# Fused cosformer attention and squared-ReLU MLP: one planner orders all engines, seven block products in the first matmul too

## The chip, the cores and the metric

The kernel runs on one NeuronCore of a Trainium2 chip. Five engines work in parallel, each through its own queue in order: TensorE (PE, matmuls, with its weight loads shown as PEld), VectorE (DVE), ScalarE (ACT), GpSimd (POOL) and SyncE (SP). In this kernel POOL and SP issue the DMA transfers, POOL on the software queue and SP on the hardware queue. Engines wait for one another on semaphores. The metric is the device time of one execution in microseconds (us).

## The reference, cut to what matters

There are 8 batches of 8 heads, 576 positions and 64 features per head. Attention is linear: both q and k go through a ReLU and are then multiplied by a cosine and by a sine of the position, which gives 128 features.

```
r = np.maximum(x, 0.0)
phi(x) = np.concatenate([r * c, r * s], axis=-1)
kv  = einsum('bhsf,bhsd->bhfd', phi(k), v);  z = sum(phi(k), axis=2)
num = einsum('bhsf,bhfd->bhsd', phi(q), kv); den = einsum('bhsf,bhf->bhs', phi(q), z) + 1e-06
x   = (num / den) as [8*576, 512]
out = (relu(x @ w_in) ** 2) @ w_out          # w_in [512, 2048], w_out [2048, 512]
```

Inputs and output are float32. The two large matmuls have 4608 x 512 x 2048 multiplications each and take nearly all of the time.

## The kernel before, in words

A batch of 576 positions is cut into four tiles of 128 (positions 4p + j, so that a partition reads whole rows) and one tail of 64. Weights are cast to bf16 by their load on the POOL queue. q, k and v come as float32, with two buffers each (`inp`, `bufs=2`), and v is cast by ACT or DVE into `vext` (`att_v`, L203 and L205), whose 65th column is 1 and so also gives z.

Per batch: features of k and q (`feat_cos` on DVE L176, `feat_sin` on ACT L186), the sums `kz` over positions (`att_kv`, L246), the copy to `kvz` (L257), the transpose of q (on PE for batches 0 and 1, by DMA from SP otherwise, L275), the numerators `num` (L318), the division on DVE (L328 to L332) and the transpose of x (PE L359 or DMA L350).

The first matmul (`gemm1`, L391) is done plainly, 16 matmuls of 256 columns into one PSUM tile `hps` (two banks, two such tiles). ACT writes relu to `rt` (L399), DVE squares into `gT` (L406). The tails of two batches are done together, 128 columns at a time.

The second matmul is plain for batch 0 (L440) and for half of batch 1 (L464). Otherwise a pair of 128-position tiles is done as a 2 x 2 block product with seven products instead of eight (`pair_mm`, L533): sums of g blocks on DVE (`g_sum`, L529), sums of w_out blocks once (`w2_sum`, L514), and the results are put together by ACT copies (L569, L584) and DVE adds (L545). A pair has four PSUM tiles `ya`, `yc`, `yv`, `yu`, one for each open sum. Tails go the same way, four batches at a time.

The order is written by hand: a list of slots (`gemm1` and `gemm2` pieces of one batch after the other), and tables (`plan`, `at`) that say behind which slot each attention piece is issued. Every engine then executes its own instructions in that order. Output goes from the POOL queue, 512 KB at a time (L418, tails L427), in the last batch from SP and ACT.

Of the kernel before, what the change touches and what calls it, by code (L numbers as in the profile page):

```python
# [14 lines left out]
EPS = 1e-06  # L15
FP = 512


@with_exitstack
def kernel(  # L20
# [15 lines left out]
    T = B * S  # L36
# [6 lines left out]
    assert P == 128 and H * D == 512 and D == 64 and TAIL == 64  # L43
    NS = J + 1

    const = ctx.enter_context(tc.tile_pool(name="const", bufs=1))
    wpool = ctx.enter_context(tc.tile_pool(name="wts", bufs=1))
    inp = ctx.enter_context(tc.tile_pool(name="inp", bufs=2))
    att = ctx.enter_context(tc.tile_pool(name="att", bufs=1))
    mlp = ctx.enter_context(tc.tile_pool(name="mlp", bufs=2))  # L50
    ps_h = ctx.enter_context(tc.tile_pool(name="ps_h", bufs=2, space=bass.MemoryType.PSUM))
    ps_y = ctx.enter_context(tc.tile_pool(name="ps_y", bufs=2, space=bass.MemoryType.PSUM))
    ps_a = ctx.enter_context(tc.tile_pool(name="ps_a", bufs=1, space=bass.MemoryType.PSUM))
# [3 lines left out]


    kqv = {}

    def load_main(src, nm, b, eng, parts=1):
        main = inp.tile([P, H, J, D], F32, name=nm, tag=nm, bufs=2)
        for i in range(parts):
            js = slice(i * J // parts, (i + 1) * J // parts)
            eng.dma_start(
                out=main[:, :, js, :],
                in_=src[b, :, 0:MAIN, :].rearrange("h (p j) d -> p h j d", j=J)[:, :, js, :],
            )
        kqv[nm, b] = main

    def load_tail(src, nm, b, eng):
        tail = inp.tile([P, HH, D], F32, name=nm + "t", tag=nm + "t", bufs=2)
        for g in range(2):
            eng.dma_start(
                out=tail[g * TAIL : (g + 1) * TAIL, :, :],
                in_=src[b, g * HH : (g + 1) * HH, MAIN:S, :].rearrange("h p d -> p h d"),
            )
        kqv[nm + "t", b] = tail

    def load_batch(b, eng, order):  # L80
        for nm in order:
            for part in (load_main, load_tail):
                part({"k": k, "v": v, "q": q}[nm], nm, b, eng)

    def piece(nm, b, j):
        return kqv[nm, b][:, :, j, :] if j < J else kqv[nm + "t", b][:, :, :]


    ident = const.tile([P, P], BF16, name="ident")
    zeros = const.tile([P, FP], BF16, name="zeros")  # L90
# [24 lines left out]


    w1sb = wpool.tile([P, KB, DFF], BF16, name="w1sb")
    w2sb = wpool.tile([P, HB, DM], BF16, name="w2sb")
# [16 lines left out]
    vexts = []  # L135
    for i in range(2):
        vx = att.tile([P, J, H, E1], BF16, name=f"vext{i}")
        vxt = att.tile([P, HH, E1], BF16, name=f"vextt{i}")
        for t in (vx, vxt):
            ones = t[:, :, :, D:E1] if t is vx else t[:, :, D:E1]  # L140
            nc.vector.memset(ones, 1.0)
        vexts.append((vx, vxt))
    kps, kvzs, kzs, qps, tqs, qpTs, xs = {}, {}, {}, {}, {}, {}, {}
    nums, xts, xtails = {}, {}, {}

    def cached(tiles, key, shape, tag, bufs):
        if key not in tiles:
            tiles[key] = att.tile(shape, BF16, name=tag, tag=tag, bufs=bufs)
        return tiles[key]


    def kp_of(b, j):
        if j == J:
            return cached(kps, (b, 1), [P, HH, F], "kpt", 1)
        return cached(kps, (b, 0), [P, J, H, F], "kp", 1)[:, j]

    def qp_of(b, j):
        if j == J:
            return cached(qps, (b, 2), [P, HH, F], "qpt", 2)
        return cached(qps, (b, j // 2), [P, 2, H, F], "qp", 2)[:, j % 2]  # L160

    def x_of(b, j):

        if j == J:
            return cached(xs, (b, 2), [P, 2, P], "xt", 2)
        return cached(xs, (b, j // 2), [P, KB, 2, P], "x", 2)[:, :, j % 2, :]

    def xT_of(b, i):
        return cached(xts, (b, i), [P, KB, 2 * P], "xT", 3)

    def xT_tails(m):

        return cached(xtails, m, [P, 2, 2, 2, TAIL], "xTt", 2)

    def feat_cos(dst, src, j):
        nc.vector.tensor_scalar(  # L176
            out=dst[:, :, 0:D],
            in0=src,
            scalar1=0.0,
            scalar2=cos_col[:, j : j + 1],  # L180
            op0=ALU.max,
            op1=ALU.mult,
        )

    def feat_sin(dst, src, j):
        nc.scalar.activation(  # L186
            out=dst[:, :, D:F], in_=src, func=ACTF.Relu, scale=sin_col[:, j : j + 1]
        )

    def feat_cos_act(dst, src, j):  # L190
        nc.scalar.activation(
            out=dst[:, :, 0:D], in_=src, func=ACTF.Relu, scale=cos_col[:, j : j + 1]
        )

    def att_k(b, j, cos=feat_cos):
        for f in (cos, feat_sin):
            f(kp_of(b, j), piece("k", b, j), j)

    def att_v(b, j, eng, h0=0, h1=H):
        copy = eng.copy if eng is nc.scalar else eng.tensor_copy  # L200
        vx, vxt = vexts[b % 2]
        if j == J:
            copy(out=vxt[:, :, 0:D], in_=piece("v", b, j))  # L203
        else:
            copy(out=vx[:, j, h0:h1, 0:D], in_=piece("v", b, j)[:, h0:h1, :])  # L205

    def warm(n):

        wm = ps_h.tile([P, 2, FP], F32, name="wm", tag="hps", bufs=2)
        for i in range(n):  # L210
            nc.tensor.matmul(
                out=wm[:, i % 2, :], lhsT=zeros[:, 0:P], rhs=zeros[:, :], start=True, stop=True
            )

    def fill(n):

        wm = ps_a.tile([P, 2, FP], F32, name="wm", tag="pa", bufs=1)
        for i in range(n):
            nc.tensor.matmul(
                out=wm[:, i % 2, :],  # L220
                lhsT=ident[:, :],
                rhs=zeros[:, :],
                start=True,
                stop=True,
            )

    def att_kv(b, part):
        vx, vxt = vexts[b % 2]
        if part == 0:
            kvzs[b] = att.tile([P, H, E1], BF16, name="kvz", tag="kvz", bufs=2)  # L230
            kzs[b] = ps_a.tile([P, 2, FP], F32, name="kz", tag="pa", bufs=1)
        kz = kzs[b]

        for j in (0, 1) if part == 0 else range(2, NS):
            for hh in range(HH):
                for half in range(2):
                    h = half * HH + hh  # L240
                    if j < J:
                        lhsT, rhs = kp_of(b, j)[:, h, :], vx[:, j, h, :]
                    else:
                        p0, p1 = half * TAIL, (half + 1) * TAIL
                        lhsT, rhs = kp_of(b, j)[p0:p1, hh, :], vxt[p0:p1, hh, :]
# [7 lines left out]
        if part == 1 and b:  # L253
            att_kvz(b, nc.scalar.copy)
# [223 lines left out]

# [337 lines left out]
```

## Time and profile before

| what | value |
|---|---|
| time, three executions | 288.13 us median (287.29 to 288.22) |
| profiled execution: first to last instruction | 286.5 us |
| median less that span (start and end of the execution) | 1.6 us |
| PE, PEld busy | 279.0, 235.6 us |
| DVE, ACT, POOL busy | 204.2, 161.8, 45.7 us |
| PE instructions | 3067 |
| data moved by DMA | 53.04 MB |

The profiled execution's own time is not given beside its span; the 1.6 us is the median's distance from the span. "Busy" is the time in which an engine had an instruction of its own under way. A matmul row's duration of 0.273 us includes its way through the array; two that follow each other start 0.109 us apart, so work on PE is counted by starts or by the chain of waits, not by durations. In the view in order of time, a bracket shows how long the engine was idle before a row and what ended that.

### The profile page before, as it was taken

What the parts mean: (1) busy time and instruction counts of PE and PEld (TensorE: products, weight loads), DVE (VectorE), ACT (ScalarE), POOL (GpSimd) and SP (SyncE); (2) the same over time, 40 slices, a digit from 0 to 9 for tenths busy, and PEclk for the clock granted to TensorE, in tenths of its full rate; (3) what the DMA queues carried; (4) which work ended last, traced back from release to release, by engine and by line L of the source; (5) the groups of instructions that cost most, each with busy time, mean ns of one, the idle gap of its engine ahead of it and who ended that gap; (6) DMA issues with size and microseconds to landing.
All of it is one profiled execution on the core that took longest, in us unless ns stands there. A gap on an engine that the chain in (4) does not pass through costs nothing.

```text
span 286.5 us, 7327 instructions
## 1 busy us (share of the span) xinstructions
PE 279.0 (97%) x3067; PEld 235.6 (82%) x3067; DVE 204.2 (71%) x457; ACT 161.8 (56%) x245; POOL 45.7 (16%) x75
## 2 busy tenths in 40 slices
PE   8899999999999999999999999999999999999995
PEld 3578855888678888889988988888988888889884
DVE  1857664688697599787598776977677877547585
ACT  3764833679669669445881458844695461155210
POOL 8925507640000000000002000000000000000002
PEclk9999999999999999999999999999999999999999
DMA  7999996999457898999439975499809620300015
GB/s 236 298 206 302 329 263 197 362 364 277 57 119 187 212 275 195 237 301 212 136 106 192 348 160 165 107 267 287 227 9 237 114 46 3 140 9 2 0 76 146
DMA packets 73825, 53.04 MB, mean 185 GB/s; under 512 B 50496, under 2 KB 68416, under 8 KB 73792
## 3 DMA queue, kind: packets, MB, share of 16 engines
q1 hardware_dynamic: 63248, 26.75, 40.4%
q0 software_dynamic: 10400, 25.69, 29.8%
q8 instruction: 24, 0.39, 0.6%
q10 hardware_dynamic: 144, 0.13, 0.1%
q14 instruction: 9, 0.07, 0.1%
HBM read 36.70 MB, written 9.44 MB: 161 GB/s over the span
## 4 chain that ended last, share of the span: by engine, by line
PE 86%; DMA 5%; POOL 3%; DVE 2%; ACT 2%; issue 1%; POOLq 0%; ACTq 0%
PE hps L391 40%; PE ya L533 9%; PE yc L533 9%; PE yu L533 7%; DMA w1sb<-in_moe_w_in_dram 5%; PE yv L533 5%; PE num L318 3%; PE kz L246 3%; PE yps L464 2%; PE yps L440 2%; PE yh L440 2%; DVE ysb L545 1%; PE tq L292 1%; POOL w1sb L122 1%; DVE u L545 1%
## 5 line engine op out<-in xcount | busy, mean ns | idle before, releaser
L391 PEld LDWEIGHTS <-w1sb 128*128 128x128 bf16 x1344 | 113.4, 98 | 13.3 <-issue 2.0
L391 PE MATMUL hps<-xT,w1sb 128*128 128x256 bf16 (+1 forms) x1088 | 119.3, 266 | 1.2 <-DMA w1sb<-in_moe_w_in_dram 0.4
L399 ACT ACTIVATE rt<-hps 128x1024 bf16<-128x1024 f32 x72 | 73.7, 1023 | 68.1 <-PE hps L391 46.7
L406 DVE TENSOR_TENSOR gT<-rt 128x1024 bf16<-128x1024 bf16 x64 | 44.0, 687 | 20.1 <-ACT rt L399 20.1
L533 PEld LDWEIGHTS <-gs 128*128 128x128 bf16 x480 | 46.9, 98 | 5.4
L418 POOL DMA_DIRECT2D out_dram<-ysb x14 | 7.6, 541 | 171.6 <-DVE ysb L545 144.9
L533 PEld LDWEIGHTS <-gT 128*128 128x128 bf16 x312 | 29.8, 98 | 3.4
L332 DVE TENSOR_TENSOR x<-num,rden 128x512 bf16<-128x512 f32 x32 | 22.1, 692 | 1.1
L186 ACT ACTIVATE kp<-k,sin_col 128x512 bf16<-128x512 f32 x32 | 22.4, 717 | 0.6 <-DMA k<-in_k_dram 0.6
L186 ACT ACTIVATE qp<-q,sin_col 128x512 bf16<-128x512 f32 x32 | 22.0, 719 | 1.1 <-DMA q<-in_q_dram 1.1
L328 DVE TENSOR_SCALAR den<-num 128x8 f32<-128x8 f32 (+1 forms) x40 | 6.6, 164 | 20.6 <-PE num L318 20.4
L529 DVE TENSOR_TENSOR gs<-gT 128x1024 bf16<-128x1024 bf16 x26 | 17.8, 684 | 0.0
L533 PE MATMUL ya<-w2t,gs 128*128 128x256 bf16 x120 | 15.6, 273 | 0.0
L533 PE MATMUL yc<-w2sb,gs 128*128 128x256 bf16 x120 | 15.6, 273 | 0.0
L533 PE MATMUL yu<-w2t,gs 128*128 128x256 bf16 x120 | 15.6, 272 | 0.0
L391 PE MATMUL hps<-xTt,w1sb 128*128 128x128 bf16 x256 | 15.1, 219 | 0.2 <-ACT rt L399 0.2
L176 DVE TENSOR_SCALAR qp<-q,cos_col 128x512 bf16<-128x512 f32 x32 | 14.7, 487 | 0.0
L533 PE MATMUL yu<-w2sb,gs 128*128 128x256 bf16 x112 | 14.5, 273 | 0.0
L205 ACT CAST vext<-v 128x512 bf16<-128x512 f32 x23 | 14.1, 614 | 0.6 <-DMA v<-in_v_dram 0.6
L584 ACT COPY s<-yu 128x256 f32<-128x256 f32 x14 | 5.2, 372 | 15.6 <-PE yu L533 15.6
L176 DVE TENSOR_SCALAR kp<-k,cos_col 128x512 bf16<-128x512 f32 x21 | 10.1, 504 | 5.0 <-DMA k<-in_k_dram 5.0
L533 PE MATMUL yc<-w2sb,gT 128*128 128x256 bf16 x104 | 13.5, 273 | 0.0
(98 smaller groups left out, 340.8 us busy)
## 6 DMA issues: line engine op xcount, KB each, us to landing
out_dram<-ysb POOLq DMA_DIRECT2D x14, 512.0 KB, 4.1
k<-in_k_dram SPq DMA_DIRECT2D x5, 1024.0 KB, 7.9
v<-in_v_dram POOLq DMA_DIRECT2D x4, 1024.0 KB, 8.6
v<-in_v_dram SPq DMA_DIRECT2D x4, 1024.0 KB, 8.7
q<-in_q_dram SPq DMA_DIRECT2D x4, 1024.0 KB, 6.7
q<-in_q_dram POOLq DMA_DIRECT2D x3, 1024.0 KB, 12.7
k<-in_k_dram POOLq DMA_DIRECT2D x3, 1024.0 KB, 10.0
w1sb<-in_moe_w_in_dram POOLq DMA_DIRECT2D x4, 512.0 KB, 11.2
```

The costliest lines, as they stand in the source:

```text
L176: nc.vector.tensor_scalar(out=dst[:, :, 0:D], in0=src, scalar1=0.0, scalar2=cos_col[:, j : j + 1], op0=ALU.max, op1=ALU.mult,)
L186: nc.scalar.activation(out=dst[:, :, D:F], in_=src, func=ACTF.Relu, scale=sin_col[:, j : j + 1])
L205: copy(out=vx[:, j, h0:h1, 0:D], in_=piece("v", b, j)[:, h0:h1, :])
L246: nc.tensor.matmul(out=kz[:, half, hh * E1 : (hh + 1) * E1], lhsT=lhsT, rhs=rhs, start=(j == 0 and hh == 0), stop=(j == J and hh == HH - 1),)
L318: nc.tensor.matmul(out=out, lhsT=lhsT, rhs=kvz[:, half * HH + hh, :], start=True, stop=True)
L332: nc.vector.tensor_tensor(out=x_of(b, j).rearrange("p (b k) (l d) -> p b k l d", b=n, l=2), in0=n4[:, :, :, 0:D].rearrange("p b (k l) d -> ...
L391: nc.tensor.matmul(out=out, lhsT=w1sb[:, kb, hb * P : (hb + 1) * P], rhs=rhs, start=(kb == 0), stop=(kb == KB - 1),)
L399: nc.scalar.activation(out=rt[:, :, :], in_=hps[:, :, :], func=ACTF.Relu)
L406: nc.vector.tensor_tensor(out=dst, in0=rt[:, :, :], in1=rt[:, :, :], op=ALU.mult)
L440: nc.tensor.matmul(out=ypss[b][tt], lhsT=gTs[b][:, hb, tt * P : (tt + 1) * P], rhs=w2sb[:, hb, :], start=(hb == 0), stop=(hb == HB - 1),)
L529: nc.vector.tensor_tensor(out=t[:, :, :], in0=in0, in1=in1, op=op)
L533: nc.tensor.matmul(out=acc, lhsT=lhs[:, hb, :], rhs=rhs[:, hb, :], start=(hb == 0), stop=(hb == HB2 - 1),)
```

## The change

All of the kernel after the first 17 us is described as operations (`Op`: possible engines with durations, what they come after, which buffers they use), and a list scheduler (`Plan.run`) puts them into one order before the program is built. Each operation has a due time; the one with the smallest due time (plus a hand-set `SHIFT`) among those ready is taken, and copies, relus, squares and features may go to ACT or DVE. Seven things come with it.

- First matmul: eight units of 512 positions x half of the hidden width (`plan_gemm1`, G2.0 to G7.0, G8.0, G8.1) take seven block products of 8 matmuls each instead of four plain blocks of 16. They need sums of w_in blocks (`w1s`, once), sums of x blocks (`xs`), three PSUM tiles `ha`, `hc`, `hb`, a copy of the first product from `ha` to `hb` ("seed"), two more copies (`s5`, `u2`) and an add with relu on DVE. The other units stay plain (`H...`).
- The tails of all eight batches form a ninth batch, b = 8, done at the end in both matmuls.
- Second matmul: every unit but those of batch 0 takes seven products (`plan_unit`, Y1.0 to Y8.1). The three open sums A, C and B lie in one PSUM tile `yac`: A and C in its first bank, B in its second. B is seeded by a copy of A.
- Features of k and q are made by one instruction each for both (1024 columns).
- v is cast by its load, which is split by tile: 4 + 2 issues a batch on POOL.
- k and q share one buffer; there is one buffer for v.
- Stores go from SP, 256 KB at a time.

The diff, cut to its core:

```diff
-    inp = ctx.enter_context(tc.tile_pool(name="inp", bufs=2))
+    pool("x", 4, True)
+    pool("kq", 1, order=1)
...
+    pool("rt", 3)
+    pool("g", 8, order=4)
+    pool("gs", 6, order=4)
+    pool("y", 2, order=1)
+    pool("ve", 1, order=1)
...
+    def load_v(b, j0, j1):
+        for j in range(j0, j1):
+            nc.gpsimd.dma_start(
+                out=vx[:, j, :, 0:D], in_=main_of("v", b)[:, :, j, :]
+            )
...
-    def pair_mm(b, pair, s):
+    def plan_unit(b, t):
+        acc = buf("x", [P, 2, FP], F32, "yac", "half")
...
+        A, C, Bb = (
+            lambda: acc[:, 0, 0:n],
+            lambda: acc[:, 0, n : 2 * n],
+            lambda: acc[:, 1, 0:n],
+        )
...
+        p1 = prod(1, A, block(0, 0), lambda: w2_block(0, 0), True, [w[0], sum5.get(b), begun.get(0)])
+        seed = ev("seed", {"ACT": act(n)}, lambda e: copy(e, Bb(), A()), [p1], [acc], 0.3)
+        p5 = prod(5, C, summed(1), lambda: w2t[1], False, [p1, w[1]])
+        c5 = ev("s5", flex, lambda e: copy(e, s5[:, :], C()), [p5], [acc, s5], 0.6)
+        p2 = prod(2, A, block(0, 1), lambda: w2_block(1, 0), False, [seed])
+        e11 = ev("c11", flex, lambda e: copy(e, y[:, 0, 0:n], A()), [p2], [acc, y], 2.0)
+        p6 = prod(6, Bb, summed(2), lambda: w2t[2], False, [seed, w[2]])
+        c2 = ev("u2", flex, lambda e: copy(e, u2[:, :], Bb()), [p6], [acc, u2], 0.3)
+        p3 = prod(3, C, summed(4), lambda: w2_block(1, 1), False, [c5])
+        e12 = ev(
+            "c12",
+            lambda e: tt(y[:, 0, n : 2 * n], C(), u2[:, :], ALU.add),
...
+        p7 = prod(7, Bb, summed(3), lambda: w2t[3], False, [c2, w[3]])
+        e22 = ev(
+            "c22",
+            lambda e: tt(y[:, 1, n : 2 * n], Bb(), s5[:, :], ALU.add),
...
+        p4 = prod(4, Bb, block(1, 1), lambda: w2t[4], False, [e22, w[4]])
+        e21 = ev("c21", flex, lambda e: copy(e, y[:, 1, 0:n], Bb()), [p4], [acc, y], 1.0)
...
+    def plan_gemm1(b, gg, xs, made):
+        a = buf("x", [P, nh, W], F32, "ha", "full")
+        c = buf("x", [P, nh, W], F32, "hc", "full")
+        bb = buf("x", [P, nh, W], F32, "hb", "seed")
...
+        def product(acc, lhs, rhs, first):
+            w, r = lhs(), rhs()
+            for i in range(nh):
+                f0 = (gg * nh + i) * P
+                for kb in range(K2):
+                    o = acc[:, i, :]
+                    mm(
+                        o.rearrange("p (b c) -> p b c", b=4) if b == B else o,
+                        w[:, kb, f0 : f0 + P],
+                        r[:, kb],
+                        first and kb == 0 and i % 2 == 0,
+                        kb == K2 - 1,
+                    )
...
+        plan.timeline(rows, 16.8)
+        plan.dues()
+        order = plan.run({"PE": 16.8, "ACT": 17.4, "DVE": 17.1, "POOL": 36.0, "SP": 1.0})
+        for o in order:
...
+            o.emit(o.engine)
```

The names below follow the planner: `G4.0.P3` is the third block product of the first matmul's unit for batch 4, first half; `Y5.1.P7` the seventh of the second matmul's unit for batch 5, second tile of each pair; `H6.1.01` a plain block; `kv3`, `num3.1`, `xT1.0` attention pieces. On PE the built order in the middle reads, for example, `Y4.1.P2 Y4.1.P6 Y4.1.P3 Y4.1.P7 Y5.0.P1 Y5.0.P5 Y4.1.P4 Y5.0.P2 Y5.0.P6 G6.0.P1 G6.0.P5 Y5.0.P3 G6.0.P2`, and near the end `G8.1.P1 Y7.0.P1 Y7.0.P5 Y7.0.P2 Y7.0.P6 Y7.0.P3 Y7.0.P7 G8.1.P2`.

## The prediction

> **What bounds the kernel now.** I read the page from the top: busy times, the span in 40 slices, then the chain that ended last.
>
> ```profile
> span 286.5 us, 7327 instructions
> PE 279.0 (97%) x3067; PEld 235.6 (82%) x3067; DVE 204.2 (71%) x457; ACT 161.8 (56%) x245; POOL 45.7 (16%) x75
> ...
> PE   8899999999999999999999999999999999999995
> ...
> PE 86%; DMA 5%; POOL 3%; DVE 2%; ACT 2%; issue 1%; POOLq 0%; ACTq 0%
> ```
>
> TensorE (PE) is busy in every slice; 86% of the chain is its work, and the DMA share is the first w_in load, which lies before 24.4 us. So time is won by fewer PE columns and lost by anything that makes PE wait. To see whether "busy" hides waits, I read stretches of 5 us (columns: PE, PEld, DVE, ACT, POOL, each with its instructions, then clock, DMA share, GB/s):
>
> ```profile
> 95.00:100.00 5.00, 5.00 (x71) 4.49 (x69) 2.69 (x6) 2.96 (x4) 0.00 (x0) 1.00 0.89 241
> 140.00:145.00 5.00, 5.00 (x60) 4.54 (x58) 3.20 (x7) 5.00 (x11) 0.00 (x0) 1.00 0.01 1
> 185.00:190.00 5.00, 4.90 (x52) 4.25 (x51) 3.41 (x10) 1.93 (x3) 0.53 (x1) 1.00 1.20 238
> ```
>
> PE stays full even where ACT is full (140 to 145), at clock 1.00. The 4.90 at 185 is one of five small holes, all at the seam between two batches. One, in order of time:
>
> ```profile
> 155.48 1.04 PE L533 MATMUL yc<-w2sb,gs 128*128 128x256 bf16 x8
> ...
> 156.35 1.04 PE L533 MATMUL yu<-w2sb,gs 128*128 128x256 bf16 x8
> ...
> 156.55 0.42 DVE L545 TENSOR_TENSOR u<-yc,u 128x256 f32<-128x256 f32 x1 [0.45 <-PE yc L533]
> 157.01 0.42 DVE L545 TENSOR_TENSOR ysb<-u,yv 128x256 f32<-128x256 f32 x1
> ...
> 157.48 0.38 PE L391 MATMUL hps<-xT,w1sb 128*128 128x256 bf16 x2
> ```
>
> It prices a hand-over. The reader of yc starts at 156.55, 0.20 after PE went on to yu (156.35). The last reader ends at 157.43 and PE restarts at 157.48, 0.05 later. PE had ended yu's eight at 156.35 + 0.87 = 157.22, so the hole is 0.26; five make 1.3 us.
>
> **PE work.** From the chain of waits and the timeline:
>
> ```profile
> 77.31 1.73 PE yps L464 x8
> ...
> 83.87 0.87 PE yu L533 x8
> ```
>
> ```profile
> 134.00 3.74 PE L391 MATMUL hps<-xTt,w1sb 128*128 128x128 bf16 x64
> ```
>
> A 256-column matmul costs 0.87/8 = 0.109, a 512-column one 1.73/8 = 0.216, a 128-column one (3.74 - 0.17 that drains behind the last) / 64 = 0.056 us. First matmul: before 960 of 256 and 384 of 128 columns, 104.8 + 21.4 = 126.2; after 608 plain + 8 units x 56 = 1056 of 256 and 64 of 128, 115.3 + 3.6 = 118.9. That is -7.3. Second: before 15 units x 56 = 840 and 96 of 512 columns, 91.7 + 20.7 = 112.4; after 16 x 56 = 896 and 64, 97.8 + 13.8 = 111.6: -0.8. Attention, transposes and warm-up keep their counts. Sum -8.1, all on the path.
>
> **Copies between products of one tile.** Before, the four sums of a unit lay in four tiles. Now A, C and B lie in one tile `yac` (A and C in its first bank, B in its second), with a copy out between most products. In the built program every such copy waits for the last product issued into the tile, not for its own product alone, and the next product into that tile waits for the copy. So two products of one unit that stand side by side on PE, with a copy between them, leave PE idle for 0.20 + 0.37 + 0.05 = 0.62 us. The 0.37 is this row:
>
> ```profile
> L569 ACT COPY s<-ya 128x256 f32<-128x256 f32 x15 | 5.6, 370 | 11.3 <-PE ya L533 9.7 <-issue 1.5
> ```
>
> If another product (0.87) stands between, the copy is hidden. I walked the built PE order and compared, at each wait, the PE work since the product waited for with hand-over plus copies. Thirteen places are bare: Y4.1 (P3, P7), Y5.1 (P3, P7), Y6.0 (P2, P6), Y7.0 (P2, P6, P3, P7), Y7.1 (P3, P7), Y8.1 (P2). Eleven at 0.62 and two at 0.65 (copy on DVE, 0.40): 8.1 us. Eight more are partly covered: two in the transposes of batch 1 behind the plain second matmul (0.84, 0.62: the slot and the x are freed by a 0.59 copy just behind), and 0.16, 0.38, 0.67, 0.51, 0.12, 0.12 between: 3.4. Sum +11.5. The same walk over the program of before finds the five holes at 0.23 each (trace: 0.26) and no other after the start, so it may be off by some 15%. The five holes go: -1.3.
>
> Weighed against a rule: the row of 157 us shows one engine waiting for another on a tile. The Trainium skill, "PSUM — Partial Sum Buffer", section "PSUM bank collisions raise a hardware error", says that a bank must be guarded against two engines at once and that another bank need not be. That speaks against putting A and C in one bank; by it alone only Y6.0.P2 and Y7.0.P2 would stay of the thirteen, and the sum below would be 284.9 instead of 291.8. The program's waits are wider than the rule, so I count thirteen. No run here shows the collision itself.
>
> **Other engines.** ACT loses 23 v casts of 0.614 and 5 of 0.40 (16.1), and 72 rows of 1.02 on `rt`; it gains 71 copies and relus and 39 squares of 1024 columns, 65 copies of 256 (0.37) and 29 double features. Priced as below that is about 190 us, DVE about 210: under 80% of the span, beside PE. Of these, the trace lacks: the double feature (512 columns take 0.717 on ACT and 0.487 on DVE; ends once and twice that; I take 1.14 and 0.75, the slope from the 256-column rows); a square on ACT (0.69, DVE's, to 1.02; I take 1.02, nearest is the relu); add-with-relu of two f32 tiles (0.69, the 1024-column bf16 row, to 1.37, twice the 512-column f32 add; I take 1.22, the slope of the f32 adds); xs sums (0.34 to 0.69; 0.42); seeds that write PSUM (0.29 to 0.45 for 256, 0.8 to 1.2 for 1024; I take the copies into SBUF, 0.37 and 1.02). These stand between products of different tiles. In the first G unit, seed, s5 and u2 end 0.5 to 1.0 before PE needs them by the built order. Where an ACT row of 1.02 is ahead in the queue, more is bare: +1.0, between 0 (copies find the queue empty) and 8 (half such a row, 0.5, at one copy of each of 16 units).
>
> **Loads.** v comes as 28 + 14 pool issues; 4 x 0.95 + 2 x 0.63 = 5.1 us of POOL a batch, where POOL is idle 84%; it is issued 13 to 25 us of PE work ahead of kv (batch 1: 9 to 11), and took 8.6. The Trainium skill, "DMA: Bandwidth & Descriptors", section "Specifications", asks for 512 bytes or more a piece, and v's are now 256; no row here has its price, and with twice the 8.6 the sum would gain about 3 at batch 1 alone. Keys and queries have one buffer instead of two. Their load is issued 9 to 13 us of PE work ahead of the first feature, and the rows say 6.7 to 12.7 from issue to landing. Stores move to SP, 40 issues of about 0.55 in the order in which their data come, 22 us in all on a queue with nothing else of that length behind them but the next loads and transposes. At the start PE reaches kv of batch 1 near 39.6, when v (before: 39.15) and the doubled features (k before: 33.9, then four rows of 1.14) are just done. I take +0.7, between -0.4 (the hole of 0.36 at 35.4 goes) and +4. The end stays: last product, a copy of 0.37 instead of an add of 0.42, and two stores on SP (-0.3 to +0.6).
>
> **Sum.** -8.1 + 11.5 - 1.3 + 1.0 + 0.7 = +3.8 on the span. The profiled span is 286.5; 1.6 lies between it and the median of 288.13, and nothing in the change touches that. 288.1 + 3.8 = 291.9; I say 291.8.
>
> **Rivals.** (1) Faster: the waits on `yac` cost little. One mechanism, at the thirteen places: the copy runs beside the next product wherever that goes to the other bank. Eleven holes go (Y6.0.P2 and Y7.0.P2 stay), -6.9, 284.9. It decides where a place costs under (8.1 - 3.8)/13 = 0.33 us. For: the copies themselves are only 0.37. Against: hand-over and restart were 0.25 in the row, and the waits stand in the program. (2) The ACT queue: every evicting copy has one 1.02 row ahead at half of its length, +8 instead of +1, 298.8. For: ACT has 8 to 10 us of work per 10 us of PE in batches 1 to 3. Against: before stood 5.00 of 5.00 at 140 to 145 without a hole. (3) Late keys and queries: landing after 12.7 instead of 8 stops ACT's features, and the copies behind them, at batches 2 and 3 by about 2 us each: 295.8. For: DMA share 1.0 to 1.2 until 70 us. Against: after that the lead grows.
>
> **How the numbers follow.** The forecast gets 0.62, with its own range 289 to 294.5; rival 1 0.13; rival 2 0.15; rival 3 0.10. The range reaches to 287.5 and 298.5: rival 1 and the upper half of rival 2 are left out, 0.2. Under 0.3% (0.9 us) this kernel's measurement can't tell. Faster 0.13 (rival 1), same 0.06 (the forecast's low edge), slower 0.81.
>
> **What would show it.** Right: PE's busy instructions near 2870, its holes on `yac` with ACT or DVE as releaser, about 0.6 each, thickest between about 175 and 275 us; none on `hc` or `ha`. Wrong: `yac` products side by side without a hole (rival 1); `yac` holes of 1 us and more with ACT full (rival 2); ACT idle before `fe` with a DMA as releaser (rival 3).

## The result and the profile after

The changed kernel takes 306.07 us (median of four, 304.82 to 307.75), the kernel before in the same comparison 287.74: ratio 1.064, 95% interval 1.059 to 1.068. Forecast were 291.8 and at most 298.5. The direction was right, the size was not: +18.3 us instead of +3.8. The profiled execution took 304.82 us, its span is 303.1, 16.6 more than before's 286.5.

From the page of the kernel after: busy times, the span in 40 slices, the chain that ended last.

```profile
span 303.1 us, 6928 instructions
PE 276.5 (91%) x2863; PEld 232.2 (77%) x2867; DVE 199.7 (66%) x389; ACT 186.4 (62%) x247; POOL 53.4 (18%) x74
...
PE   8599999499979999999999999899988999979991
...
PEclk9989999869999999999999999999999999999998
...
PE 76%; DMA 11%; ACT 5%; DVE 3%; issue 1%; POOL 1%; SPq 0%; POOLq 0%; DVEq 0%; ACTq 0%
```

PE has 2863 instructions, as forecast (near 2870). But it is no longer busy in every slice: there is a hole in the eighth slice (53 to 61 us) with a slow clock just behind it, dips around 80 to 90 us, and a wider band of shallow ones late. The chain has 11% DMA where it had 5%, and 5% ACT where it had 2%.

Stretches of 5 us (columns as in the prediction: PE, PEld, DVE, ACT, POOL, then clock, DMA share, GB/s), first before, then after:

```profile
40.00:45.00 5.00, 5.00 (x58) 2.86 (x57) 1.04 (x4) 1.38 (x3) 0.09 (x1) 1.00 1.01 281
55.00:60.00 5.00, 5.00 (x59) 4.47 (x57) 4.60 (x11) 3.13 (x4) 2.14 (x3) 1.00 1.03 360
```

```profile
40.00:45.00 5.00, 4.37 (x66) 3.12 (x65) 0.81 (x2) 2.67 (x3) 2.56 (x4) 1.00 1.63 199
...
55.00:60.00 5.00, 1.38 (x8) 0.70 (x7) 3.69 (x6) 3.71 (x4) 0.00 (x0) 0.86 1.61 137
60.00:65.00 5.00, 3.73 (x21) 2.76 (x21) 3.87 (x5) 4.72 (x9) 0.00 (x0) 0.50 1.12 196
```

Before, the DMA engines are at a share of 1.0 and move 281 to 360 GB/s in these two stretches. After, the share of packet time is 1.6 and only 137 to 199 GB/s arrive. From 55 to 60 us PE stands for 3.6 of 5 us, and the next 5 us run at half clock (0.50).

For a ledger I took, from the rows of the trace, the time from the start of each matmul to the start of the next, less the median of its form; what exceeds 0.03 us is lost time, holes and slow clock alike (own count, us; the last three columns are experiments, below).

```
stretch        before   after   no cross-bank   and no v from   and no v from
                                waits           batch 2 on      batch 1 on
0 to 40          5.5      7.7       7.3             7.8             7.5
40 to 50         0.2      1.5       1.9             2.3             0.2
50 to 70         0.9      7.7       7.8             7.7             5.5
70 to 90         0.4      3.6       3.0             0.7             0.5
90 to the end    4.0     13.2       6.4             5.3             5.3
sum             11.0     33.6      26.4            23.8            19.0
```

The rest of PE's time, the work itself, is 268.8 before and 260.1 after (-8.7). From PE's last end to the end of the span it is 3.4 us before (283.08 to 286.46) and 5.7 after (297.36 to 303.05). So -8.7 + 22.6 + 2.3, and +0.4 in pieces under 0.03 and rounding, make the 16.6.

**The late part, 90 us on (+9.2).** All thirteen bare places of the forecast are there, 0.62 to 0.75 each, 8.43 together. Unit Y7.0 in the timeline of the kernel after (start, duration, instruction, idle time before it and what ended it):

```profile
265.24 1.04 PE L516 MATMUL yac<-w2t,gs 128*128 128x256 bf16 x8
...
266.37 0.36 ACT L487 COPY yac<-yac 128x256 f32<-128x256 f32 x1 [1.31 <-PE yac L516]
...
266.78 1.03 PE L516 MATMUL yac<-w2sb,gT 128*128 128x256 bf16 x8 [0.50 <-ACT yac L487]
...
268.40 1.03 PE L516 MATMUL yac<-w2t,gs 128*128 128x256 bf16 x8 [0.58 <-DVE ys L487]
...
269.47 0.37 ACT L487 COPY y<-yac 128x256 f32<-128x256 f32 x1 [1.82 <-PE yac L516]
...
269.89 1.03 PE L516 MATMUL yac<-w2sb,gs 128*128 128x256 bf16 x8 [0.46 <-ACT y L487]
```

The first copy here is the seed, P5 (265.24) is ahead of it, and four products in a row wait for a copy. The copy at 269.47 starts 0.20 behind P6's last column (268.40 + 0.87) and P3 starts 0.05 behind the copy: the same hand-over that the prediction priced at the seam of before.

**The early part, up to 90 us (+13.5).** The chain of waits of the kernel after, 39 to 67 us:

```profile
39.68 0.40 SPq L553
...
40.13 16.05 DMA kq<-in_q_dram
...
56.29 4.27 ACT fe L503 x4
60.55 0.48 ACT xT L487
...
61.07 0.60 PE tx L651 x4
...
61.70 0.59 ACT xT L487
...
62.33 3.39 PE hps L516 x16
65.72 1.21 PE kz L516 x40
```

The queries of batch 2 are issued at 40.13 and take 16.05 us. Four double features follow on ACT, 4.27 together, and in ACT's order copies of the transposed x of batch 1 stand behind them, which PE needs; other such copies stand behind features on DVE. PE idles 2.98 us before 58.77 and 1.72 before 61.07. The sixteen matmuls at 62.33 then take 3.39 us instead of 1.91 (16 x 0.109 + 0.17), at half clock. The waits of the kernel after say the same by engine (total, times, longest):

```profile
ACT fe L503 <- DMA kq<-in_q_dram: 9.0, 4, 6.4
...
DVE fe L505 <- DMA kq<-in_k_dram: 5.9, 2, 5.6
...
DVE fe L505 <- DMA kq<-in_q_dram: 5.4, 3, 4.1
```

The planner's own model of the order has batch 2's first feature at 51.45 and starts its sums `kz` at 59.97. In the trace they start at 65.6. Before started them at 73.9: the new order wants these sums some 14 us earlier than the old one had them, and got them 8 us earlier. The model books 4.0 us of the DMA engines for a batch's main v and 3.1 for its keys or its queries (`plan_loads`).

What the DMA engines carry, from the pages' third part, before and then after:

```profile
DMA packets 73825, 53.04 MB, mean 185 GB/s; under 512 B 50496, under 2 KB 68416, under 8 KB 73792
```

```profile
DMA packets 106528, 48.89 MB, mean 161 GB/s; under 512 B 83296, under 2 KB 100704, under 8 KB 106496
```

There are 4 MB less, in 44% more packets. From the records of single packets (own count): v's cast pieces are 128 bytes as written and take 31 to 32 ns each, 4096 of them a batch, which is 8.2 us of all 16 engines, twice the 4.0 that the planner books. Before, a megabyte of v came as 256 packets of 4096 bytes and 160 to 195 ns, 2.6 to 3.1 us. In the kernel after, v of batch 1 fills 36 to 42 us, the last two w_out loads lie at 40 to 50 (before they are done by 44), and batch 2's keys and queries at 42 to 55.5, beside them and beside v of batch 2.

The largest hole between 70 and 90 us (2.06 in the ledger) has another cause than late keys and queries. Batch 3's features wait only 0.5 us for theirs from 60 to 90. In the timeline of the kernel after:

```profile
87.36 0.43 DVE L513 TENSOR_TENSOR xs<-xT 128x512 bf16<-128x512 bf16 x1 [2.79 <-DMA xT<-xp]
...
87.71 0.68 DVE L513 TENSOR_TENSOR gs<-gT 128x1024 bf16<-128x1024 bf16 x1
...
88.45 1.05 PE L516 MATMUL yac<-w2t,gs 128*128 128x256 bf16 x8 [1.89 <-DVE gs L513]
```

The chain of waits has a DMA transpose of x, from 77.21, which takes 10.13 us where the median of these transposes is 4.0. Until about 85 us the DMA records show v of batch 3 beside it, in its 128-byte packets. DVE's sums of x wait for it, a sum of g blocks stands behind them on DVE, and PE waits for that.

The Trainium skill, "DMA: Bandwidth & Descriptors", section "Specifications", asks for 512 bytes or more a piece. The packets agree in direction, by bytes as written: 128 bytes in 31 ns is 4 bytes a nanosecond, 4096 bytes in 160 to 195 is 21 to 26.

### The profile page after: what moved, and what is told of

Same layout as the page of the kernel before. It is cut to its first block, busy times and chain, and to the rows that moved or that the text cites. A ratio compares the mean times of both kernels' runs of the same rounds, so it can differ in the third digit from the quotient of the medians.

```text
span 303.1 us, 6928 instructions
## 1 busy us (share of the span) xinstructions
PE 276.5 (91%) x2863; PEld 232.2 (77%) x2867; DVE 199.7 (66%) x389; ACT 186.4 (62%) x247; POOL 53.4 (18%) x74
## 4 chain that ended last, share of the span: by engine, by line
PE 76%; DMA 11%; ACT 5%; DVE 3%; issue 1%; POOL 1%; SPq 0%; POOLq 0%; DVEq 0%; ACTq 0%
PE yac L516 33%; PE hps L516 20%; DMA kq<-in_q_dram 8%; PE hb L516 7%; PE ha L516 4%; PE hc L516 4%; DMA xT<-xp 3%; ACT fe L503 3%; PE num L516 3%; PE kz L516 2%; ACT y L487 1%; DVE fe L505 1%; PE tx L651 1%; DVE y L513 1%; PE wm L516 1%
## 5 line engine op out<-in xcount | busy, mean ns | idle before, releaser
L516 PEld LDWEIGHTS <-w1sb 128*128 128x128 bf16 x864 | 81.4, 99 | 11.2 <-issue 1.1
L516 PE MATMUL hps<-xT,w1sb 128*128 128x256 bf16 (+1 forms) x672 | 77.1, 271 | 0.9 <-ACT rt L491 0.6
L497 ACT ACTIVATE gT<-rt 128x1024 bf16<-128x1024 bf16 x39 | 41.2, 1056 | 9.7 <-DVE rt L510 5.6
L564 POOL DMA_DIRECT2D vext<-in_v_dram x28 | 25.6, 926 | 121.1 <-PE kz L516 117.7
L491 ACT ACTIVATE rt<-hps 128x1024 bf16<-128x1024 f32 x33 | 33.5, 1019 | 16.6 <-PE hps L516 16.3
L516 PE MATMUL yac<-w2sb,gs 128*128 128x256 bf16 x256 | 33.0, 272 | 3.7 <-ACT yu L487 1.8
L516 PE MATMUL yac<-w2t,gs 128*128 128x256 bf16 x256 | 32.4, 273 | 3.3 <-DVE gs L513 1.9
L516 PE MATMUL yac<-w2sb,gT 128*128 128x256 bf16 x256 | 33.1, 273 | 1.8 <-ACT yac L487 1.0
L516 PEld LDWEIGHTS <-w1s 128*128 128x128 bf16 x256 | 24.8, 98 | 2.8
L513 DVE TENSOR_TENSOR gs<-gT 128x1024 bf16<-128x1024 bf16 x32 | 21.7, 687 | 2.0 <-ACT gT L497 1.6
L634 DVE TENSOR_TENSOR xp<-num,den 128x512 bf16<-128x512 f32 x32 | 22.1, 692 | 1.1
L487 ACT COPY y<-yac 128x256 f32<-128x256 f32 x29 | 10.7, 369 | 18.3 <-PE yac L516 10.8
L516 PE MATMUL yac<-w2t,gT 128*128 128x256 bf16 x128 | 16.6, 272 | 0.8 <-DVE y L513 0.7
L516 PE MATMUL hb<-xs,w1s 128*128 128x256 bf16 x128 | 16.6, 273 | 0.0
```

The costliest lines, as they stand in the source:

```text
L487: (nc.scalar.copy if e == "ACT" else nc.vector.tensor_copy)(out=out, in_=in_)
L491: nc.scalar.activation(out=out, in_=in_, func=ACTF.Relu)
L497: nc.scalar.activation(out=out, in_=in_, func=ACTF.Square)
L513: nc.vector.tensor_tensor(out=out, in0=in0, in1=in1, op=op)
L516: nc.tensor.matmul(out=out, lhsT=lhsT, rhs=rhs, start=start, stop=stop, skip_group_check=True)
L564: nc.gpsimd.dma_start(out=vx[:, j, :, 0:D], in_=main_of("v", b)[:, :, j, :])
```

## The experiments

My theory after the result had two parts: (a) the tile-wide waits on `yac` cost the late part, and (b) v's small packets fill the DMA engines and make keys and queries late. Rivals to (b) were the single buffer of k and q, the order in which SP and POOL issue, and the place of the features in ACT's order. The kernel before stood at 287.7 to 288.5 us in all comparisons; ratios are against it. What v's small pieces alone would cost in the order of the kernel before has not been measured.

### 1. Waits between banks dropped

Products into one bank of `yac` and copies out of the other are declared independent; waits within a bank stay.

```diff
+        def free_of(insts, bank, pe_side):
+            for other, bank2, pe2 in done:
+                if bank2 != bank and pe2 != pe_side:
...
+                            tc.declare_no_dep(x, o, reason="other bank")
...
+                    int(m in (6, 7, 4)),
...
+                if nm != "seed":
+                    free_of([i], int(nm in ("u2", "c22", "c21")), False)
```

> The changed kernel, with the waits between products and copies of one yac tile dropped where they lie in different PSUM banks (A and C against B); the waits inside one bank stay. Theory A (the step of the prediction on copies between products): 11 of the 13 bare places close, only Y6.0.P2 and Y7.0.P2 stay at about 0.62, one P3 keeps 0.2; the walk over the built order gives 13.6 us of bare waits with the old waits and 6.3 with the new. So 306.1 - 7.3 = 298.8, range 298 to 299.8, and the holes at 223 to 231, 266 to 271, 279 to 281 and 295 us are gone from the trace. Rival (the holes are there but what follows them soaks them up, as late x or features take their place): 303 to 306. In both cases the holes at 55 to 65 and 80 to 90 us stay.

Measured: 298.56 us (297.38 to 299.94), ratio 1.036 (1.032 to 1.040), 7.5 less than with the waits. The same unit Y7.0 in this kernel's timeline:

```profile
264.71 1.04 PE L516 MATMUL yac<-w2t,gs 128*128 128x256 bf16 x8
...
264.98 0.43 DVE L487 COPY ys<-yac 128x256 f32<-128x256 f32 x1 [2.13 <-PE yac L516]
...
265.44 0.37 ACT L487 COPY y<-yac 128x256 f32<-128x256 f32 x1 [0.73 <-DVE ys L487]
265.78 0.37 ACT L487 COPY yu<-yac 128x256 f32<-128x256 f32 x1
265.86 1.91 PE L516 MATMUL yac<-w2sb,gs 128*128 128x256 bf16 x16
```

P6, P3 and P7 follow one another (264.71, then from 265.86 sixteen in a row), with the copies beside them; only 0.28 is still lost ahead of P3. Eleven of the thirteen holes are gone; the two P2 that follow P1 and the seed closely stay (0.66 each), as the prediction said of the bank rule taken by itself. Part (a) is shown: the late stretch falls from 13.2 to 6.4 in the ledger. The early part is untouched.

### 2. v in pieces of 512 bytes

v is loaded in one transfer a batch into a side buffer, from which POOL copies it into `vext`.

```diff
-        for j in range(j0, j1):
-            nc.gpsimd.dma_start(
-                out=vx[:, j, :, 0:D], in_=main_of("v", b)[:, :, j, :]
-            )
+        nc.gpsimd.dma_start(out=vst[:, :, :, :], in_=main_of("v", b))
...
+        for j in range(J if b else 0):
+            nc.gpsimd.tensor_copy(out=vx[:, j, :, 0:D], in_=vst[:, :, j, :])
-    pool("g", 8, order=4)
+    pool("g", 7, order=4)
```

> The changed kernel, with v of batches 1 to 7 cast by one load a batch into a side buffer (1 KB read, 512 B written a piece, a fourth of the pieces) and copied from there on POOL, four copies a batch; the order on all other engines is the same. Theory B (the small v pieces hold up the keys and queries that share the 16 DMA engines): the queries of batch 2, issued at 41, land near 49 to 51 instead of 56.3, the holes at 55 to 66 us (about 7 with the slow clock after them) go and those at 80 to 90 (about 2.5) shrink: 297 to 300. Rival C (the total traffic or the late issue behind the single buffer does it, whatever the pieces): the queries still land at 55 or later, 304 to 307. Rival D: the sums of keys and values wait for the POOL copies (each 1 to 2 us, four in a row) and give part of it back at batch 1, +2 to +4 at 43 us.

Measured: 313.14 us (312.24 to 313.49), ratio 1.086 (1.083 to 1.089), 7 more than the changed kernel. Each packet is 512 bytes and 59 ns, 3.8 us of the engines a batch instead of 8.2, and yet the queries of batch 2 took longer (chain of waits of this kernel):

```profile
39.75 17.21 DMA kq<-in_q_dram
...
68.15 0.64 SPq L664
...
69.48 12.05 DMA kq<-in_q_dram
```

The next keys and queries, which SP issues behind its transposes of batch 2's queries, went out at 68.9 instead of 63.4, because those transposes took 8.47 us, and batch 3 became late (holes of 4.55 at 55.8 and 6.46 at 79.1). (b) as I had put it, with piece size as the one cause, fell. The run adds POOL copies and takes one `g` buffer away, so it doesn't measure the size of the pieces alone.

### 3. Features of batch 2 put later in the order

```diff
+        late = [o for o in order if o.name in [f"{f}2.{j}" for f in ("cos", "sin") for j in range(J)]]
+        late += [o for o in order if o.name in ("qTd2.0", "qTd2.1")]
+        order = [o for o in order if o not in late]
+        at = next(i for i, o in enumerate(order) if o.name == "xTc1.3") + 1
+        order[at:at] = late
```

> The changed kernel, with the eight features of batch 2 (and the two DMA transposes of its queries) moved behind the copies of the four x transposes of batch 1 on ACT and DVE; all else in the same order. Theory E (the hole at 55 to 62 us is ACT and DVE standing in order behind features that wait for a late load, with x copies of batch 1 queued behind them): x of batch 1 is there by 55, the first matmul of batch 1 starts near 57 instead of 62.3, and 3 to 6 us are won: 300 to 303; part comes back at the sums of keys and values of batch 2 (before: 65.6), which still wait for the same features. Rival F (the late load bounds what comes next in any order): PE stops at those sums instead, for as long: 305 to 307.

Measured: 309.93 us (308.96 to 310.9), ratio 1.076 (1.072 to 1.081), slower than either theory had it. Of the hole at 56 us 0.84 is left, and one of 3.50 stands at 59.8, ahead of batch 2's sums, another of 3.58 at 79.1. The place of the features in ACT's order is where the wait shows, not where it comes from: moved behind, they make the sums late instead.

### 4. Keys and queries on POOL's queue, with and without v in large pieces

Both on top of experiment 1. The first issues the main loads of k and q from POOL, behind v; the second has v as in experiment 2 too.

```diff
-                lambda e, nm=nm: load_main(nm, b, queue(e)),
+                lambda e, nm=nm: load_main(nm, b, nc.gpsimd),
```

> e1_banks, with the main loads of keys and queries of batches 2 to 7 issued from POOL's queue instead of SP's. In the DMA records of the changed kernel, POOL's f32 loads travel as packets of 4096 B (about 160 ns each, 2.6 us of all 16 engines for 1 MB), SP's as packets of 1024 B (59 ns, 3.8 us), and SP's packets take turns with the w_out and v packets of the other queue. Theory G (keys and queries of batch 2 come late because they share the DMA engines packet by packet with w_out and v): behind w_out and ahead of v in one queue they land near 51 to 52.5 instead of 56.3; the hole at 55 to 62 shrinks by 3 to 5, the one at 80 to 90 by 1 to 2; 291 to 295. Rival C (the DMA engines are full until then in any order; only the landing order changes): queries land at 55 or later, or w_out or v come late in their place; 297 to 300.

> e5_kq_pool, with v of batches 1 to 7 in large pieces through a side buffer and POOL copies, as in e2_vbig. v's packets of 128 B written cost 31 ns each, 4096 of them 8 us of all 16 engines a batch; of 512 B 59 ns, 1024 of them 3.8 us. Theory G with the pieces (what is saved now comes ahead of nothing that is waited for, except v of batch 1 and 2): v of batch 1 lands 1 to 2 us earlier and closes part of the wait at 42 to 44, v of batch 2 near 56; 1 to 3 us faster than e5. Rival D (the POOL copies, 0.57 to 0.8 each, and the loads queued behind them on POOL cost as much): the same as e5 or 1 to 4 slower.

Measured: 314.62 to 321.53 us for the first (its executions lie too far apart for a ratio); 322.54 (320.18 to 324.5), ratio 1.120 (1.113 to 1.126) for the second. Some 24 us more than experiment 1 in the second. Its chain of waits:

```profile
59.39 18.02 DMA qpT<-fe
...
117.35 17.71 DMA qpT<-fe
```

Two DMA transposes of queries, which take 4.6 us from issue to landing in the median of the changed kernel, took 18 beside k and q on the other queue. That trades one late transfer for another. The single packets fit this: POOL's packets of k and q are 4096 bytes and 159 to 187 ns, those of a transpose 256 bytes and mostly 18 ns, and both are served in the same stretch in like numbers (143 and 141 from 66 to 68 us).

### 5. v left out, from batch 2 on, and from batch 1 on

Both on top of experiment 1; the second differs in `b > 0`.

```diff
     def load_v(b, j0, j1):
+        if b > 1:
+            return
         for j in range(j0, j1):
```

> e1_banks, without the main loads of v from batch 2 on (the sums of keys and values use the v of batch 1 in their place; the v tails are still loaded). This leaves all of v's share in the lateness out from batch 2 on. Theory B' (v's 4096 small pieces a batch are what holds up keys and queries): queries of batch 2 land near 51, and the holes at 55 to 66 and 80 to 90 go almost wholly: 289 to 292. Rival C' (batch 2's queries are late by w_out, keys and queries themselves; v only takes what is left): they land at 54 or later, and 1 to 3 us are won: 295.5 to 298.

> As the run that dropped the cross-bank waits and left out v's main loads from batch 2 on (294.44 us), and here v's main load of batch 1 is left out too; only that of batch 0 stays, so the outputs of the later batches are computed with batch 0's v and are not the reference's. It tells what makes batch 2's queries late, which in that run still landed 16.1 us after their issue at 40.4. Theory N (full DMA engines: v of batch 1, 4096 packets of 31 to 32 ns, 8.2 us of all 16 engines at 36 to 42, pushes the last two w_out loads to 40 to 50, and these share the engines with batch 2's keys and queries): w_out is done by about 44, the queries of batch 2 land about 11 us after issue, near 51, where the plan has its first feature (51.45); the holes of 2.75 and 2.08 between 55 and 62 and the clock of 0.50 to 0.57 behind them go; 288.5 to 290.5 us. Rival P (the single buffer: the load can only be issued at 40, when batch 1's features are done, and two loads of 1 MB need 14 us or more whatever else is on the engines): the queries land at 54.5 or later, the holes stay, 293 to 294.5 us.

Measured: 294.44 us (293.55 to 294.9), ratio 1.022 (1.019 to 1.025), and 289.78 (289.24 to 290.88), ratio 1.007 (1.004 to 1.009). In the chain of waits of the first, then of the second:

```profile
40.41 16.10 DMA kq<-in_q_dram
...
56.61 4.27 ACT fe L503 x4
```

```profile
40.95 11.99 DMA kq<-in_q_dram
...
53.05 4.27 ACT fe L503 x4
...
58.89 3.43 PE hps L516 x16
```

Without v from batch 2 on, the time falls by 4.1 us, and batch 2's queries are as late as ever, as rival C' had it. What goes is the dip at 70 to 90 (ledger 3.0 to 0.7), the one behind the late transpose of x.

Without v of batch 1 it falls by another 4.7 us. The ledger puts 2.1 of this at 40 to 50 us and 2.2 at 50 to 70. The first part is v's own landing: in the first run PE stands 0.92 and 0.65 us for `vext` in batch 1's sums, in the second not at all. The second part is batch 2's queries, which land after 11.99 us instead of 16.10. With v of batch 1, its packets are over at about 43, just when the first ones of those keys and queries start, so it delays them through others: the last two w_out loads are now done at 46.3 instead of 51.3 in experiment 1, and the keys and queries run nearly alone at 44 to 48 us (665 and 686 packets in 2 us, against 241 to 309 in the changed kernel, experiment 1 and the first run here). By these records v of batch 1 delays w_out, and w_out shares the engines with batch 2's queries. With the waits (7.5), these three steps take 16.3 of the 18.3 us away.

The time is in theory N's range, its signs only in part: the queries still land at 52.9, 1.6 later than the plan's 51.35, and 5.5 us remain in the ledger at 50 to 70 (a hole of 2.08 at 55.7, one of 0.88, and slow clock). The single buffer and the early plan may be the cause; no run shows it. The two runs leave v out altogether; how much of the 8.8 is the size of its packets, and how much any load of v would cost at that place, they don't tell.

### 6. Half of the last tails' stores from POOL

On top of experiment 1; the same stores alternate between SP and POOL.

```diff
-            nc.sync.dma_start(out=dst, in_=y[g * TAIL : (g + 1) * TAIL, i, :])
+            (nc.gpsimd if g else nc.sync).dma_start(
+                out=dst, in_=y[g * TAIL : (g + 1) * TAIL, i, :]
+            )
```

> e1_banks, with the second half of each store of the last tokens issued from POOL instead of SP. In the changed kernel six stores stand in a row on SP from 295.0 to 299.4 (0.73 each) and the last product ends at 297.4. Theory H (the end is the row of issues on SP): the last issue ends 0.5 to 1.2 earlier; 297.4 to 298.1. Rival I (the transfer's own latency of 2.5 to 3.6 after the last copy sets the end, from either queue): the same within 0.4.

Measured: 296.68 us (296.33 to 299.75), ratio 1.033 (1.027 to 1.040); experiment 1 had 1.036 (1.032 to 1.040), so the intervals don't part them. The spans differ by 1.4, but the end itself, from PE's last end, only went from 5.7 to 5.4 (289.56 to 294.93). In the changed kernel SP's row of six issues (0.73 each, 295.02 to 299.42) ends 1.1 behind the last copy. With the row split between two queues, the end is nearly as long: that it is the row was not borne out. From the last issue to the end it is 3.6 in both kernels and 2.55 before; why, stays open.

### 7. v held back until the queries are there

On top of 6, v in large pieces and each load of v from batch 2 on behind a tiny POOL copy that reads the last query of the same batch.

```diff
+        if b > 1:
+            nc.gpsimd.tensor_copy(out=seen[:, 0:1], in_=kq[b][:, 1, H - 1, J - 1, D - 1 : D])
+        nc.gpsimd.dma_start(out=vst[:, :, :, :], in_=main_of("v", b))
```

> e8_tail, with v in large pieces (as in e2_vbig) and, from batch 2 on, v's load held on POOL until the queries of the same batch have landed (a copy of one of their elements on POOL stands ahead of it). Theory J (what makes batch 2 late is the sum of what lies ahead of or beside its queries on the DMA engines: v of batch 1 in small pieces, which pushes the last w_out loads to 42 to 50, and then v of batch 2): with 3.8 instead of 8 us for v of batch 1 and v of batch 2 out of the way, the queries land near 53 instead of 56.3, v of batch 2 near 57; the holes at 55 to 66 shrink by 3, those at 80 to 90 by 2: 290.5 to 293 against 296.7. Rival K (the order of e2 again: large pieces let v, w_out and the DMA transposes of the queries fight for the queue, and the loads of batch 3 behind them on SP come later): 297 to 310.

Measured: 297.44 us (296.28 to 298.78), ratio 1.033 (1.028 to 1.037), no better than without. The queries of batch 2 land after 13.66 us, and lost time at 50 to 70 falls from 8.3 to 5.4. But v then runs beside the transposes, which take 7.42, the next keys are issued at 66.1, and 70 to 90 rises from 2.6 to 5.1.

### 8. A second buffer for batch 2's keys and queries

On top of 6, batch 2's k and q go into the room of the w_in sums, which are made later, and are issued at 30 instead of 40 us. The second kernel also issues batch 3's ahead of the transposes. The third is the first with v in large pieces.

```diff
+        kq[2].tile = sb.tile(kq[2].shape, kq[2].dtype, name="kq", tag="w1s", bufs=1)
+        move(["ldk2", "ldq2"], "ldqt2.1")
...
+        move(["ldk3", "ldq3"], "ldvt2")
```

> e8_tail, with a buffer of its own for the keys and queries of batch 2: it lies where the sums of w_in blocks come later, and these sums (four on DVE, 1.22 each) are moved from 26 to 40 us to between 63 and 80 us. Its loads are issued on SP behind the key and query tails, at about 32 instead of 40, with nothing to wait for. Theory L (the prediction's third rival: with one buffer the load can't be issued before batch 1's last feature, and the chain of waits runs from there through the queries' load): the queries of batch 2 land near 48 to 50 instead of 56, features follow at once, the sums of keys and values come at 60 to 62 instead of 68 (PE's holes at 55 to 66 were 8), and the total is 289 to 293; the sums of w_in on DVE may take back 1 to 2. Rival M (the DMA engines are full from 20 to 57 us, share 1.1 to 1.8 in every stretch, so that an earlier issue only makes w_out or v of batch 1 late): the hole moves to 42 to 50 us, 295 to 298.

> e10_two, with the loads of keys and queries of batch 3 also issued earlier on SP: behind the tails and v of batch 2, ahead of the DMA transposes of batch 2's queries (their buffer has been free since batch 1's features). Theory L: batch 3's features no longer wait (the holes at 78 to 90 us were 2.3 to 2.6): 1 to 3 us less than e10. Rival M: they come beside v and the transposes and make these late: the same as e10 or up to 3 more.

> e10_two, with v of batches 1 to 7 in large pieces through a side buffer and POOL copies, as in e2_vbig. In e10's DMA records from 40 to 46 us the two queues take turns packet by packet (about 460 of v's 128 B against 460 of the queries' 1024 B in each 2 us), so v of batch 1 with its 4096 packets lands at 51.5. Theory M' (packets take turns, so that v's number of packets sets when it lands beside another load): with 1024 packets it lands near 42 to 44, the sums of batch 1 come at 45 to 47 instead of 52, the holes at 40 to 50 us (8.3) shrink by 5 to 7, and the early queries of batch 2 now pay: 291 to 296. Rival M (the engines are full, whatever the pieces): w_out or the queries come late in its place, and the holes stay above 6 in all between 40 and 66: 298 to 303.

Measured: 302.36 us (301.81 to 304.69), ratio 1.051 (1.045 to 1.057); 302.05 (301.32 to 302.3), ratio 1.048 (1.045 to 1.050); and for the third four times from 299.46 to 308.07, too far apart for a ratio. Chain and stretches of the first:

```profile
33.87 17.65 DMA vext<-in_v_dram
51.51 0.04 issue
51.56 0.93 PE kz L516 x16
```

```profile
40.00:45.00 5.00, 1.75 (x21) 1.05 (x19) 1.15 (x3) 1.68 (x2) 1.64 (x2) 0.91 1.34 272
45.00:50.00 5.00, 0.60 (x8) 0.49 (x8) 0.00 (x0) 0.00 (x0) 0.87 (x1) 0.50 1.63 194
```

The queries are in time (issued at 31.0, landed 17.4 later), and v of batch 1 now takes 17.65 us where v's issues took 10.0 in the median of the changed kernel, so that batch 1's sums wait: the hole moves from 56 to 43, and is larger. For the third, no conclusion is drawn. In the second kernel the holes at 80 to 90 go and v's tails land still later (18.80 us). In these runs the second buffer changed which transfer is late, not whether one is.

## Why the prediction was right and wrong

- **PE work, -8.1:** right, -8.7 measured. This was counted from matmuls and their row durations.
- **Copies between products of one tile, +11.5, and the seam holes, -1.3:** right in place and mechanism. The thirteen places measured 8.43 against 8.1. The partly covered ones (3.4) are not settled one by one: two are plain in the trace (0.78 and 0.68), and the whole late stretch grew by 9.2, against 10.2 of both terms and 11.2 with ACT's +1.0, though some of the covered places lie before 90 us. Rival 1 (the waits cost little) is refuted: the holes are there, and taking their waits away gave 7.5. What it said would be left of the thirteen, two P2, is left, with 0.28 at one P3.
- **Rival 2, ACT's queue:** no sign of it. ACT is busy 62%, and PE's waits have no row on `ha`, `hc` or `hb`.
- **Loads, +0.7, bounds -0.4 to +4: this step failed.** It set the margin from issue to need (9 to 13 us) against landing times of before (6.7 to 12.7) and called that enough. Batch 2's queries took 16.05, and up to 90 us the ledger has 13.5 more than before: 2.2 up to 40, 1.3 at 40 to 50, 6.8 at 50 to 70 behind these queries, 3.2 at 70 to 90, most of it behind a transpose of x that took 10.13. The landing times of before belong to before's traffic: fewer packets, w_out done by 44, and batch 2's sums not before 73.9. Leaving v out from batch 1 on takes 8.8 us away.
- The prediction weighed the rule on pieces of 512 bytes at v's own landing, "about 3 at batch 1 alone". At that place it is small: the last row of batch 1's sums starts at 43.98 against 43.28 before, with 0.54 of waiting for v (1.4 in experiment 1). The larger part is paid by other transfers on the same engines: w_out, and with it batch 2's queries, and the transpose of x. I also gave the pieces as 256 bytes; written as bf16 they are 128.
- **Rival 3, late keys and queries, 295.8:** right in mechanism at batch 2, with the sign that was named (ACT idle before `fe`, a DMA as releaser). It put 2 us each on batches 2 and 3. The ledger has 6.8 more at 50 to 70; the 3.2 more at 70 to 90 are mostly the transpose of x, which no rival named. "DMA share 1.0 to 1.2 until 70 us" was in its favour, and I gave it 0.10. Its 295.8 is the forecast, `yac` holes included, with 4 us on top: the right addition, and too small.
- **The end, 0:** wrong by 2.3. The prediction counted two stores on SP; six stand there in a row, but splitting them gave only 0.3. About 0.4 is the add and the copy one behind the other behind the last product (297.46 to 298.29, before one add), and the rest lies behind the last data; its cause is not settled.
- **Slow clock:** not foreseen. It adds about 1.5 us at 62 us behind the hole (3.39 for sixteen matmuls instead of 1.91).
- **The start:** 0 to 40 us lost 2.2 us more than before in the changed kernel (7.7 against 5.5), and 6.3 to 9.7 in all versions of the new order. None of the runs tested why.

No version here beats the kernel before. The lowest that computes everything is that of experiment 6, at 296.68.

## What to carry to other kernels

A transfer's time from issue to landing, read from the kernel before, holds only while packets, neighbours and the time of need stay the same: count packets times their duration over 16 engines for each stretch, all queues together, and ask who stands behind a transfer that becomes dearer. Where the DMA engines were full here, giving one late transfer more room made the next one late (experiments 4, 7 and 8), and putting its users later moved the wait (experiment 3); of what was tried on the loads, only leaving v out helped. Copies out of one tile that stand between products into it cost a hand-over and the copy each (0.62 here) even where they touch different banks, when the program's waits are kept per tile (experiment 1).

## What the runs showed of the hardware

- **Two queues with work were served in near-equal numbers of packets, whatever the packets' size.** In the first kernel of experiment 8, from 40 to 46 us, each 2 us had 447 to 475 packets of v (128 bytes) and 457 to 471 of k and q (1024 bytes). The Trainium skill, "DMA: Bandwidth & Descriptors", section "Queues, rings and completion order", says that each engine goes round its queues packet by packet. The near-equal counts agree. So v's queue moved an eighth of the other's bytes here. The transposes of 18 us beside 4096-byte packets (experiment 4) fit that.
- **Duration of a packet by what it writes** (own count): 256 bytes of a transpose 18 to 31 ns, 128 of a cast 31, 512 of a cast 59, 1024 of k and q from SP 46 to 59, 1024 of a w_out cast 96 to 98, 4096 of a plain POOL load 160 to 195.
- **The clock and idle time.** PE idle for 1.06 us (before, at 9.65) and for 1.89 (after, at 86.5) left the clock at 1.00. Idle for 2.98 and 1.72 with 0.6 of work between, at 55.8 to 61, was followed by 0.50 from 60 to 65; 2.53 and 1.06 at the start of the kernel after by 0.74 from 15 to 20; 0.71 and 1.92 at 54.8 to 57.8 in the last run of experiment 5 by 0.86 from 55 to 60 and 0.80 from 60 to 65. So one idle stretch of 1.9 us alone left the clock, and one of 1.9 with 0.7 just ahead of it did not.
- **v's first landing** differs by up to 2.5 us between kernels with the same start (its first cast starts at 9.96 to 12.44 us, 11.46 in the changed kernel; PE's first block of the first matmul at 17.6 to 21.7).
